# The state-space scan of a Mamba-2 block ahead of a routed MoE, laid out anew

## The chip, the cores and the metric

The kernel runs on 1 core of one Trainium2 chip. The metric is the device time of one launch in microseconds (us): 385.34 as the median of 3 runs of the kernel before (384.26 to 385.63). TensorE has two clock levels, 1.2 and 2.4 GHz; the profile gives the granted clock as a share of full speed.

## The reference, cut to what matters

```
# x [4, 8, 768, 32], a [4, 8, 768], B, C [4, 8, 768, 16]: batch, head, step, ...
# chunks of 64 steps, per (batch, head):
cum   = cumsum(log(clip(a, 1e-6, 1)))                 # within a chunk
L     = exp(cum_i - cum_j) for i >= j, else 0
y     = (L * (C @ B^T)) @ x                           # inside a chunk
S'    = exp(cum_end) * S + (exp(cum_end - cum) * B)^T @ x    # state [16, 32]
y    += exp(cum) * C @ S                              # from the chunks before
tokens = y as [3072, 256]                             # heads side by side
e      = (token_id * 2654435761) % 8                  # expert of a token
out    = relu(tokens @ W1[e]) @ W2[e]                 # 256 -> 1024 -> 256, fp32
```

All data are fp32. There are 4 batches of 12 chunks of 64 steps and 8 heads, so 384 small scan problems, and then 8 experts with some 384 tokens each.

## The kernel before, in words

The kernel has two halves. The **scan** writes y to a DRAM tensor `y_tokens`; the **MoE** gathers the tokens of one expert at a time from it (L454), turns them (L477), multiplies with W1 and W2 (L489, L498), turns back (L515) and scatters the rows to the output (L459). The MoE is the same in both kernels, but for the moments at which weights are loaded.

In the scan a "chunk" of the program (`chunk(gc)`, 24 of them, 6 in a batch) is 128 steps, two of the reference's chunks, u = 0 and 1, one in each half of the partitions. Once a batch `prepare(b)` makes the operands:

- B and C lie as 128 rows of 6 steps each; DVE multiplies them with the decay factors (`rows`, L330), PE turns them with 12 transposes (L337), and ACT and DVE copy them out of PSUM (L340 to L344). `bt` and `ce` then have head and state (8 x 16) on the partitions and the steps along the row. `ce` has three copies: C of the even heads, of the odd heads, and whole.
- B is turned back by 6 transposes (L348) so that its steps lie on partitions, and 24 matmuls (L359) make the state that each 64 steps add, all 8 heads at once, of which 4 x 4 blocks of heads are computed and the diagonal is used. DVE runs the recurrence over 12 states (L372) and masks each one to the diagonal (`up`, L375).

A chunk has 8 "grams" (L393: 64 x 64 decayed C B^T for two heads each, 8 tiles of PE), a causal mask by DVE (`m`, L396), 4 "z" matmuls (L405, the part from the earlier states), copied to SBUF by ACT (L407), 16 "y" matmuls (L413), and DVE's sum of the two (L416), which one DMA writes out (L417).

Once, after the second chunk, `invert()` (L293 to L316) turns the expert slots of the tokens into lists for the gathers: two POOL operations on one-hot tables (L302, L304) and 24 matmuls (L307).

What sets the order: the functions are called in the order of the loop at L419 to L440, and a scheduler then arranges the instructions on each engine by its own estimates. One SP queue issues all loads and the writes of y; POOL issues the gathers and scatters. There are five weight buffers (`NWB = 5`); L109 and L111 load W1 and W2 of an expert.

Of the kernel before, what the change touches and what calls it, by code (L numbers as in the profile page):

```python
# [9 lines left out]
F32 = mybir.dt.float32  # L10
# [10 lines left out]
def kernel(  # L21
# [11 lines left out]
    nc = tc.nc  # L33
# [12 lines left out]
    NWB = 5  # L46
# [27 lines left out]
    awork = pool(a_ctx, "awork", 2)  # L74
    ps_t = pool(a_ctx, "ps_t", 2, space=PSUM)
    ps_g = pool(a_ctx, "ps_g", 2, space=PSUM)
    ps_y = pool(a_ctx, "ps_y", 2, space=PSUM)


    a_t = apre.tile([P, SQ], F32)  # L80
    nc.sync.dma_start(out=a_t, in_=a.rearrange("b h (q t) -> (b h q) t", q=Q))
# [39 lines left out]
    causal = const.tile([P, G, HL], F32)  # L121
    for u in range(2):
        nc.vector.tensor_copy(out=causal[u * HL:(u + 1) * HL],
                              in_=upto[0:HL, 0:HL].unsqueeze(1).to_broadcast([HL, G, HL]))
    turn0 = const.tile([P, UQ, HL], F32)
    nc.vector.memset(turn0, 1.0)
    nc.vector.memset(turn0[:, :, 0:1], 0.0)
# [15 lines left out]
    selq = const.tile([P, Q, BH], F32)
    nc.vector.tensor_copy(out=selq, in_=ident.rearrange("p (j q) -> p q j", q=Q))
    mbq = apre.tile([P, NB, Q], F32)
    nc.vector.tensor_reduce(out=mbq, in_=idv.rearrange("p b h q -> p b q h"), axis=AX.X, op=OP.add)
    mh = apre.tile([P, H], F32)
    nc.vector.tensor_reduce(out=mh, in_=idv.rearrange("p b h q -> p h b q"), axis=AX.XY, op=OP.add)
    mhn = apre.tile([P, H, NS], F32)
    nc.vector.tensor_copy(out=mhn, in_=mh.unsqueeze(2).to_broadcast([P, H, NS]))  # L150
# [4 lines left out]
    cum = apre.tile([P, UQ, HL], F32)  # L155
    nc.vector.tensor_tensor_scan(out=cum.rearrange("p u t -> p (u t)"), data0=turn0.rearrange("p u t -> p (u t)"),
                                 data1=a_t, initial=0.0, op0=OP.mult, op1=OP.add)
    mid = cum[:, :, HL // 2 - 1:HL // 2]
    rel = apre.tile([P, UQ, HL], F32)
    nc.vector.tensor_tensor(out=rel, in0=cum, in1=mid.to_broadcast([P, UQ, HL]), op=OP.subtract)  # L160
    fac = apre.tile([P, 2, SQ], F32)
    relf = rel.rearrange("p u t -> p (u t)")
    nc.scalar.activation(fac[:, 0], relf, AF.Exp, scale=-1.0)
    nc.scalar.activation(fac[:, 1], relf, AF.Exp)
    fac_ps = ps_t.tile([P, 2, R, BH], F32, name="tp")
    for i in range(2):
        for r in range(R):
            for q in range(Q):
                nc.tensor.matmul(out=fac_ps[q * PQ:(q + 1) * PQ, i, r],
                                 lhsT=fac[:, i].rearrange("p (t r) -> p r t", r=R)[:, r], rhs=selq[:, q],  # L170
                                 start=True, stop=True)
    dec = const.tile([P, 2, R, BH], F32)
    nc.vector.tensor_copy(out=dec, in_=fac_ps)

    ends = apre.tile([P, 2, UQ], F32)
    nc.vector.tensor_copy(out=ends[:, 0], in_=mid.rearrange("p u o -> p (u o)"))
    nc.vector.tensor_copy(out=ends[:, 1], in_=rel[:, :, HL - 1])
    endb = apre.tile([P, 2, NB * Q, UQ], F32)
    for i in range(2):
        nc.vector.tensor_tensor(out=endb[:, i], in0=ends[:, i].unsqueeze(1).to_broadcast([P, NB * Q, UQ]),  # L180
                                in1=mbq.rearrange("p b q -> p (b q)").unsqueeze(2).to_broadcast([P, NB * Q, UQ]),
                                op=OP.mult)
    end_ps = ps_t.tile([P, 2, NB, NU], F32, name="tp")
    nc.tensor.matmul(out=end_ps.rearrange("p i b u -> p (i b u)"), lhsT=mhn.rearrange("p h n -> p (h n)"),
                     rhs=endb.rearrange("p i c u -> p (i c u)"), start=True, stop=True)
    step = const.tile([P, NB, NU], F32)
    nc.vector.tensor_copy(out=step, in_=end_ps[:, 0])
    nc.vector.tensor_tensor(out=step[:, :, 1:], in0=step[:, :, 1:], in1=end_ps[:, 1, :, 0:NU - 1], op=OP.add)
    nc.scalar.activation(step, step, AF.Exp)
# [22 lines left out]
    def routing():  # L212

        assert E == 8 and 2654435761 % E == 1
# [24 lines left out]

        start = route.tile([P, E], F32)  # L240
# [7 lines left out]
                                op0=OP.logical_shift_right)  # L248
        tiles = route.tile([P, E], F32)
# [5 lines left out]

        base = route.tile([P, E], F32)
# [358 lines left out]
```

## Time and profile before

| | us |
|---|---|
| median of 3 runs | 385.34 |
| the profiled execution | 384.65 |
| its span, first to last instruction | 382.9 |
| first y leaves (L417) | 29.9 |
| last y leaves (L417) | 159.93 |
| first matmul of expert 0 (L489) | 170.72 |

The span has three stages: start and scan (0 to 159.93), the first gathers (to 170.72), and the MoE. Two of PE's records per fp32 matmul are to be expected: it is done in two passes, so a count of 768 at L413 is 384 matmuls. The mean duration of a matmul record includes time in which other tiles of PE run beside it; what a group costs is read from its start to the start of the next group. The `PEclk` row is the granted clock where the trace has a record of it.

### The profile page before, as it was taken

What the parts mean: (1) busy time and instruction counts of PE and PEld (TensorE: products, weight loads), DVE (VectorE), ACT (ScalarE), POOL (GpSimd) and SP (SyncE); (2) the same over time, 40 slices, a digit from 0 to 9 for tenths busy, and PEclk for the clock granted to TensorE, in tenths of its full rate; (3) what the DMA queues carried; (4) which work ended last, traced back from release to release, by engine and by line L of the source; (5) the groups of instructions that cost most, each with busy time, mean ns of one, the idle gap of its engine ahead of it and who ended that gap; (6) DMA issues with size and microseconds to landing.
All of it is one profiled execution on the core that took longest, in us unless ns stands there. A gap on an engine that the chain in (4) does not pass through costs nothing.

```text
span 382.9 us, 5947 instructions
## 1 busy us (share of the span) xinstructions
PE 330.9 (86%) x2375; PEld 214.2 (56%) x2375; DVE 126.5 (33%) x328; ACT 67.6 (18%) x142; POOL 71.7 (19%) x85
## 2 busy tenths in 40 slices
PE   2688688999898888549999999999999999999950
PEld 2466557778776776525555555555555555555520
DVE  6769644544733453111121211212122131211210
ACT  3500043043034211101111011010110201111110
POOL 2001400000000000074212605216043120211230
PEclk9999999999999855557999999999999999999985
DMA  9977564739440000122033441432011000000100
GB/s 163 168 122 230 157 176 90 223 92 268 154 132 29 15 29 29 41 74 63 27 127 123 128 164 55 144 123 68 4 43 43 14 27 0 29 14 0 45 27 16
DMA packets 50256, 33.29 MB, mean 87 GB/s; under 512 B 35087, under 2 KB 46505, under 8 KB 50228
## 3 DMA queue, kind: packets, MB, share of 16 engines
q1 hardware_dynamic: 47412, 26.34, 26.0%
q0 software_dynamic: 2816, 6.56, 5.4%
q8 instruction: 19, 0.31, 0.3%
q14 instruction: 9, 0.07, 0.1%
HBM read 26.60 MB, written 6.55 MB: 87 GB/s over the span
## 4 chain that ended last, share of the span: by engine, by line
PE 57%; issue 17%; DMA 7%; DVE 7%; POOL 5%; SPq 2%; ACT 2%; POOLq 0%; DVEq 0%
PE h_ps L489 15%; PE o_ps L498 14%; PE y_ps L413 9%; DMA out_dram<-o_sb,idx_out 5%; PE gram L405 5%; PE tp L359 4%; PE gram L393 4%; POOL out_dram L459 2%; PE tp L337 2%; DVE m L396 2%; SPq L94 2%; PE tp L348 2%; PE xt_ps L477 1%; DMA bc<-in_B_dram 1%; DVE v L372 1%
## 5 line engine op out<-in xcount | busy, mean ns | idle before, releaser
L489 PE MATMUL h_ps<-xT,w 128*128 128x416 f32 x256 | 102.4, 525 | 0.4 <-DVE xT L478 0.4
L498 PE MATMUL o_ps<-hT,w 128*128 128x416 f32 x256 | 102.1, 518 | 0.0
L498 PEld LDWEIGHTS o_ps<-hT,w 128*128 128x128 f32 x256 | 47.5, 190 | 40.1 <-issue 36.3
L489 PEld LDWEIGHTS h_ps<-xT,w 128*128 128x128 f32 x256 | 47.4, 195 | 32.7 <-issue 31.5
L413 PE MATMUL y_ps<-x_t,m 64*64 64x32 f32 x768 | 64.0, 287 | 0.0
L413 PEld LDWEIGHTS y_ps<-x_t,m 64*64 64x64 f32 x768 | 60.1, 215 | 0.0
L459 POOL DMA_INDIRECT out_dram<-o_sb,idx_out x32 | 31.2, 975 | 114.1 <-ACT o_sb L518 95.8
L454 POOL DMA_INDIRECT xg<-y_tokens,idx_in x32 | 32.0, 1000 | 94.4 <-issue 63.5
L405 PE MATMUL gram<-up,ce 64*64 64x128 f32 x192 | 34.0, 437 | 12.8 <-DVE m L396 10.5
L484 DVE TENSOR_SCALAR hT<-h_ps 128x416 f32<-128x416 f32 x32 | 18.9, 592 | 75.1 <-PE h_ps L489 75.1
L478 DVE COPY xT<-xt_ps 128x256 f32<-128x256 f32 (+1 forms) x32 | 12.0, 375 | 71.1 <-PE xt_ps L477 71.1
L482 ACT ACTIVATE hT<-h_ps 128x416 f32<-128x416 f32 x32 | 16.5, 517 | 97.3 <-PE h_ps L489 97.3
L405 PEld LDWEIGHTS gram<-up,ce 64*64 64x64 f32 x192 | 16.7, 204 | 23.3 <-DVE m L396 15.4
L407 ACT ACTIVATE z_sb<-gram 128x128 f32<-128x128 f32 x48 | 13.2, 277 | 88.7 <-PE gram L405 64.5
L393 PE MATMUL gram<-ce,bt 32*64 32x128 f32 x384 | 25.9, 435 | 0.0
L416 DVE TENSOR_TENSOR y_sb<-y_ps,z_sb 128x256 f32<-128x256 f32 x24 | 10.2, 424 | 38.5 <-ACT z_sb L407 22.8
L477 PEld LDWEIGHTS xt_ps<-ident,xg 128*128 128x128 f32 (+1 forms) x64 | 8.4, 148 | 21.7 <-issue 19.6
L359 PE MATMUL tp<-x_t,bs 64*64 64x128 f32 x192 | 20.0, 427 | 0.0
L477 PE MATMUL xt_ps<-ident,xg 128*128 128x128 f32 (+1 forms) x64 | 12.6, 280 | 8.5 <-issue 6.6
L396 DVE TENSOR_TENSOR m<-gram,causal 128x256 f32<-128x256 f32 x48 | 18.9, 417 | 3.2 <-PE gram L393 3.1
L375 DVE SCALAR_TENSOR_TENSOR up<-v,step,own 128x128 f32<-128x128 f32 x44 | 18.9, 429 | 0.5
L359 PEld LDWEIGHTS tp<-x_t,bs 64*64 64x64 f32 x192 | 16.0, 217 | 2.0 <-issue 1.3
(117 smaller groups left out, 186.6 us busy)
## 6 DMA issues: line engine op xcount, KB each, us to landing
w<-in_moe_w_dram SPq DMA_DIRECT2D x16, 1024.0 KB, 5.7
x_t<-in_x_dram SPq DMA_DIRECT2D x24, 128.0 KB, 4.2
y_tokens<-y_sb SPq DMA_DIRECT2D x24, 128.0 KB, 1.8
bc<-in_B_dram SPq DMA_DIRECT2D x4, 384.0 KB, 4.5
bc<-in_C_dram SPq DMA_DIRECT2D x4, 384.0 KB, 4.8
xg<-y_tokens,idx_in POOLq DMA_INDIRECT x32
out_dram<-o_sb,idx_out POOLq DMA_INDIRECT x32
a_t<-in_a_dram SPq DMA_DIRECT2D x1, 96.0 KB, 2.1
```

The source lines that it names most:

```text
L359: nc.tensor.matmul(out=d_ps[u][q * HL:(q + 1) * HL, c - c0], lhsT=bs[u * HL:(u + 1) * HL, c, q * HL:(q + 1) * HL], rhs=xs[b * R + c][u * H ...
L375: nc.vector.scalar_tensor_tensor(out=up[:, k + 1].rearrange("p g d -> p (g d)"), in0=v, scalar=step[:, b, k + 1:k + 2], in1=own.rearrange( ...
L393: nc.tensor.matmul(out=gram[u * HL:(u + 1) * HL, k, 0:P], lhsT=bt[r, t], rhs=ce[r, 0:2, t], start=True, stop=True)
L396: nc.vector.tensor_tensor(out=m.rearrange("p (k e) i -> p k (e i)", k=2), in0=gram[:, :, 0:P], in1=causal.rearrange("p (k e) i -> p k (e i ...
L405: nc.tensor.matmul(out=gs[q][u * HL:(u + 1) * HL, 0, P:2 * P], lhsT=ce[rq, 2, t], rhs=up[rq, 2 * c + u].rearrange("p g d -> p (g d)"), sta ...
L413: nc.tensor.matmul(out=y_ps[w, h * D:(h + 1) * D], lhsT=ms[q][w, k], rhs=x_t[w, h], start=True, stop=True)
L454: nc.gpsimd.indirect_dma_start(out=dst, out_offset=None, in_=y_dram[:], in_offset=bass.IndirectOffsetOnAxis(ap=idx, axis=0), bounds_check= ...
L459: st = nc.gpsimd.indirect_dma_start(out=out[:], out_offset=bass.IndirectOffsetOnAxis(ap=idx, axis=0), in_=src, in_offset=None, bounds_chec ...
L477: nc.tensor.transpose(out=tp[:, i, 0:r], in_=g[0:r, i * P:(i + 1) * P], identity=ident[0:r, 0:r])
L484: nc.vector.tensor_scalar_max(out=o, in0=i, scalar1=0.0)
L489: nc.tensor.matmul(out=hp, lhsT=w1s[e][:, i, f * P:(f + 1) * P], rhs=xT[e][:, i], start=(i == 0), stop=(i == DP - 1))
L498: nc.tensor.matmul(out=oP[e][:, j, 0:CAP], lhsT=w2s[e][:, f, j * P:(j + 1) * P], rhs=h, start=(f == 0), stop=(f == FP - 1))
```

## The change

The scan is written anew between the loads and `a_ctx.close()`; the same sums are formed from other tiles.

- **Order.** A manual schedule holds around the scan: instructions stay on each engine as the program has them. The grams of the next chunk come before the outputs of this one; a preparation of the next batch is spread over the six chunks of a batch, the routing over some twenty.
- **Loads.** B and C lie as 96 rows of 8 steps (512-byte pieces) in one buffer, x by head with the heads 0 to 3 in the lower 64 partitions and 4 to 7 in the upper (8 DMAs a batch in place of 6; 16 for the first batch), a as 96 rows with pieces of 32 bytes.
- **B by steps.** The decayed B goes from SBUF to a DRAM tensor and comes back with steps on partitions (`put_steps`, `get_steps`); the 6 transposes that turned it back and their copies go. C and B take 8 transposes of 96 rows each.
- **States.** 44 matmuls per batch of 32 x 64 outputs (pairs of heads) in place of 24 of 64 x 128; DVE's recurrence works on 64 columns; POOL masks them in two operations (`blocks`).
- **Grams.** Still 8 matmuls per chunk, but both u of a pair of heads go to the same partitions, side by side; four tiles of PE in place of eight. One DVE operation masks all.
- **Outputs.** z is the first matmul of a PSUM accumulation and y is added to it; the two head halves have a bank each. One ACT copy replaces two ACT copies and a DVE sum. Two DMAs write it.
- **Start.** Matmuls on constants (`spin`) stand between the first operations of PE.
- **Weights.** Four buffers in place of five.

The diff, cut to its core:

```diff
-    NWB = 5
+    NWB = 4
-    ps_y = pool(a_ctx, "ps_y", 2, space=PSUM)
+    ps_y = pool(a_ctx, "ps_y", 1, space=PSUM)
+    scan_order = tc.manual_schedule()
+    scan_order.__enter__()
+    a_t = apre.tile([NR, BH, RS], F32)
+    nc.sync.dma_start(out=a_t, in_=a.rearrange("b h (p r) -> p (b h) r", r=RS))
...
+    def load_x(b, parts=1):
+        t = aload.tile([P, NU, G, D], F32, name="x_t", bufs=3)
+        for u in range(parts):
+            us = slice(u * NU // parts, (u + 1) * NU // parts)
+            for h in range(H):
+                q, k = divmod(h, G)
+                nc.sync.dma_start(out=t[q * HL:(q + 1) * HL, us, k],
+                                  in_=x[b, h].rearrange("(u j) d -> j u d", j=HL)[:, us])
...
+    def spin(moving, n=1):
+        t = ps_y.tile([P, 2, 512], F32, name="y_ps")
+        for _ in range(n):
+            nc.tensor.matmul(out=t[:, 0, 0:moving.shape[-1]], lhsT=ident[0:moving.shape[0]], rhs=moving, ...)
+    spin(ones, 10)
...
+    def rows(b, i, eng):
+        t = abat.tile([NR, RS, P], F32, name="rows", bufs=2)
+        eng.tensor_tensor(out=t.rearrange("p r (h n) -> p h r n", h=H), in0=bcs[b][:, i],
+                          in1=fac[:, i, b * H:(b + 1) * H].unsqueeze(3).to_broadcast([NR, H, RS, NS]), op=OP.mult)
+    def put_steps(b):
+        nc.sync.dma_start(out=b_dram[b].rearrange("(p r) n -> p r n", r=RS), in_=rws[b, 0])
+    def get_steps(b):
+        t = abat.tile([P, NU, HL], F32, name="bs")
+        for q in range(2):
+            nc.sync.dma_start(out=t[q * HL:(q + 1) * HL],
+                              in_=b_dram[b].rearrange("(k j) (q n) -> q j k n", j=HL, q=2)[q])
...
+    def turned(b, i):
+        t = rws.pop((b, i))
+        for r0 in (0, RS // 2):
+            tp = ps_t.tile([P, 512], F32, name="tp")
...
+                nc.tensor.transpose(out=v[:, r], in_=t[:, r0 + r], identity=ident[0:NR, 0:NR])
...
+    def turn_c(b):
+        ct = abat.tile([P, NU, RS, RU], F32, name="ct", bufs=1)
+        for r0, v in turned(b, 1):
+            nc.scalar.activation(ct[:, :, r0:r0 + RS // 2].rearrange("p k r c -> p r k c"), v, AF.Copy)
...
+        for e in range(2):
+            nc.vector.tensor_scalar(out=ce[:, e], in0=c3, scalar1=par[:, e:e + 1], scalar2=None, op0=OP.mult)
+        nc.gpsimd.tensor_tensor(out=cp, in0=c3, in1=step[:, b].unsqueeze(2).to_broadcast([P, NU, HL]), op=OP.mult)
+    def states(b, half):
+        for i in range(n):
+            k = half * UH + i
+            for r in range(G):
+                q, g = divmod(r, 2)
+                w = slice(q * HL, (q + 1) * HL)
+                nc.tensor.matmul(out=tp[32 * r:32 * r + 32, i * PW:(i + 1) * PW], lhsT=bs[w, k, 32 * g:32 * g + 32],
+                                 rhs=xb[w, k, 2 * g:2 * g + 2].rearrange("p h d -> p (h d)"), start=True, stop=True)
...
+                nc.vector.scalar_tensor_tensor(out=st[:, k + 1], in0=st[:, k], scalar=step[:, b, k:k + 1],
+                                               in1=tp[:, i * PW:(i + 1) * PW], op0=OP.mult, op1=OP.add)
+    def blocks(b, k0, k1):
+        nc.gpsimd.tensor_tensor(out=ups[b][:, k0:k1], in0=sts[b][:, k0:k1]..., in1=own..., op=OP.mult)
...
-        for q in range(2):
-            gram = ps_g.tile([P, 2, 512], F32, name="gram")
-            for k in range(2):
-                r = slice(32 * (2 * q + k), 32 * (2 * q + k) + 32)
-                for u in range(2):
-                    nc.tensor.matmul(out=gram[u * HL:(u + 1) * HL, k, 0:P], lhsT=bt[r, t], rhs=ce[r, 0:2, t], ...)
+    def grams(gc):
+        gram = ps_g.tile([P, 2, 512], F32, name="gram")
+        for u in range(2):
+            for r in range(G):
+                q, g = divmod(r, 2)
+                rr = slice(32 * r, 32 * r + 32)
+                nc.tensor.matmul(out=gram[q * HL:(q + 1) * HL, g, u * P:(u + 1) * P],
+                                 lhsT=bts[b][rr, 2 * c + u].rearrange("p c r -> p (c r)"), rhs=ces[b][rr, :, 2 * c + u], ...)
+        nc.vector.tensor_tensor(out=m..., in0=gram[:, :, 0:2 * P], in1=causal..., op=OP.mult)
+    def outputs(gc):
+        y_ps = ps_y.tile([P, 2, 512], F32, name="y_ps")
+        for q in range(2):
+            for u in range(2):
+                if k:
+                    nc.tensor.matmul(out=y_ps[u * HL:(u + 1) * HL, q, 0:P], lhsT=cps[b][w, k],
+                                     rhs=ups[b][w, k].rearrange("p g x -> p (g x)"), start=True, stop=False)
+        for h in range(G):
+            for q in range(2):
+                for u in range(2):
+                    nc.tensor.matmul(out=y_ps[u * HL:(u + 1) * HL, q, h * D:(h + 1) * D], lhsT=m[w, g, u, e],
+                                     rhs=xs[b][w, k, h], start=(k == 0 and h == 0), stop=(h == G - 1))
+        nc.scalar.activation(y_sb, y_ps[:, :, 0:P], AF.Copy)
+        for u in range(2):
+            t0 = gc * P + u * HL
+            nc.sync.dma_start(out=y_dram[t0:t0 + HL, :].rearrange("(p r) d -> r p d", r=RS),
+                              in_=y_sb[u * HL:(u + 1) * HL].rearrange("p q d -> p (q d)"))
...
+    for gc in range(NCH):
+        if gc + 1 < NCH:
+            grams(gc + 1)
+        outputs(gc)
+        if gc == 0:
+            states(0, 1)
+            blocks(0, UH + 1, NU)
+        next(todo, None)
+        if c == 0:
+            rows(nb, 0, nc.gpsimd)
+            rows(nb, 1, nc.gpsimd)
+            if nb + 1 < NB:
+                load_x(nb + 1)
+        elif c == 1:
+            put_steps(nb)
+            turn_b(nb)
+            if nb + 1 < NB:
+                load_bc(nb + 1)
+        elif c == 2:
+            get_steps(nb)
+            turn_c(nb)
+        elif c == 3:
+            states(nb, 0)
+        elif c == 4:
+            states(nb, 1)
+            blocks(nb, 1, UH + 1)
+            if b == 1:
+                load_w(0)
+            elif b == 2:
+                load_w(1)
+        else:
+            blocks(nb, UH + 1, NU)
+    for _ in todo:
+        pass
+    load_w(2)
```

How PE's order moves. First PE in the kernel before, in the first batch, after the inversion: grams (L393), transposes for the preparation (L337, L348), z (L405), y (L413) and states (L359).

```order
L393 MATMUL gram<-ce,bt 64x128 x8
L337 MATMUL tp<-ident,rows 128x128
L405 MATMUL gram<-up,ce 64x128 x2
L413 MATMUL y_ps<-x_t,m 64x32 x5
L405 MATMUL gram<-up,ce 64x128 x2
L413 MATMUL y_ps<-x_t,m 64x32 x11
L337 MATMUL tp<-ident,rows 128x128 x5
L393 MATMUL gram<-ce,bt 64x128
L337 MATMUL tp<-ident,rows 128x128 x3
L393 MATMUL gram<-ce,bt 64x128
L337 MATMUL tp<-ident,rows 128x128 x3
L393 MATMUL gram<-ce,bt 64x128 x6
```

And PE in the changed kernel, from the second chunk of batch 1 on: z is L471, y L480, grams L454, transposes L389, states L426.

```order
L454 MATMUL gram<-ce,bt 64x128 x8
L471 MATMUL y_ps<-up,cp 64x128 x4
L480 MATMUL y_ps<-x_t,m 64x32 x16
L389 MATMUL tp<-ident,rows 128x96 x8
L454 MATMUL gram<-ce,bt 64x128 x8
L471 MATMUL y_ps<-up,cp 64x128 x4
L480 MATMUL y_ps<-x_t,m 64x32 x16
L389 MATMUL tp<-ident,rows 128x96 x8
L454 MATMUL gram<-ce,bt 64x128 x8
L471 MATMUL y_ps<-up,cp 64x128 x4
L480 MATMUL y_ps<-x_t,m 64x32 x16
L426 MATMUL tp<-x_t,bs 32x64 x24
```

In the kernel before, the grams of a chunk are directly followed by its own z and y, which need the mask made of them; now a whole chunk's z and y stand between the grams and the outputs that need them, and the transposes and states of the next batch stand between two chunks.

SP in the kernel before, in the first batch: the writes of y (L417) with the loads of x (L94), weights (L109, L111) and B and C (L88) among them.

```order
L417 DMA y_tokens<-y_sb 128x256
L94 DMA x_t<-in_x_dram 128x8x32
L109 DMA w_974<-in_moe_w_dram 128x2x1024
L417 DMA y_tokens<-y_sb 128x256
L94 DMA x_t<-in_x_dram 128x8x32 x2
L417 DMA y_tokens<-y_sb 128x256
L111 DMA w_976<-in_moe_w_dram 128x8x256
L88 DMA bc<-in_B_dram 128x8x96
L88 DMA bc<-in_C_dram 128x8x96
L417 DMA y_tokens<-y_sb 128x256
```

SP in the changed kernel, over the first batch: L487 writes y, L373 puts the decayed B of the next batch into DRAM, L379 fetches it by steps.

```order
L487 DMA y_tokens<-y_sb 8x8x256 x2
L101 DMA x_t<-in_x_dram 64x12x32 x8
L487 DMA y_tokens<-y_sb 8x8x256 x2
L373 DMA b_steps<-rows 96x1024
L90 DMA bc<-in_B_dram 96x8x128
L90 DMA bc<-in_C_dram 96x8x128
L487 DMA y_tokens<-y_sb 8x8x256 x2
L379 DMA bs<-b_steps 64x12x64 x2
L487 DMA y_tokens<-y_sb 8x8x256 x4
```

The round trip of B stands between writes of y: the put behind the second chunk's, the get behind the third's, and the get waits on this queue for the put to land.

## Rows read from the trace of the kernel before

**Rows 1.** The profile's page: its first line and the granted clock in 40 slices.

```profile
span 382.9 us, 5947 instructions
...
PEclk9999999999999855557999999999999999999985
```

**Rows 2.** Stretches: length, busy (x) of PE, PEld, DVE, ACT, POOL; PEclk, DMA, GB/s.

```profile
0.00:29.90 29.90, 18.21 (x221) 13.41 (x221) 20.11 (x79) 10.52 (x16) 2.24 (x17) 1.00 0.87 146
29.90:71.65 41.75, 34.01 (x394) 26.60 (x391) 24.51 (x50) 8.74 (x18) 6.08 (x3) 1.00 0.63 177
71.65:159.93 88.28, 78.41 (x1129) 64.50 (x1124) 40.66 (x113) 21.52 (x52) 0.20 (x1) 0.84 0.32 95
159.93:170.72 10.79, 2.40 (x9) 1.19 (x9) 1.50 (x4) 0.00 (x0) 6.21 (x6) 0.50 0.22 64
170.72:382.90 212.18, 197.85 (x632) 108.45 (x632) 39.73 (x84) 26.81 (x56) 56.99 (x58) 0.96 0.18 59
```

**Rows 3.** Timeline of one chunk: start, us, engine, line, records [idle before <-releaser].

```profile
113.74 0.48 PE L405 MATMUL gram<-up,ce 64*64 64x128 f32 x2
...
116.29 0.73 PE L393 MATMUL gram<-ce,bt 32*64 32x128 f32 x16
...
116.95 0.47 PE L337 MATMUL tp<-ident,rows 128*128 128x128 f32 x1
117.06 0.75 DVE L396 TENSOR_TENSOR m<-gram,causal 128x256 f32<-128x256 f32 x2 [0.18 <-PE gram L393]
...
117.54 0.48 PE L405 MATMUL gram<-up,ce 64*64 64x128 f32 x2
```

**Rows 4.** Timeline of PE where four and where eight of its tiles work together.

```profile
116.29 0.52 PE L393 MATMUL gram<-ce,bt 32*64 32x128 f32 x8
...
5.29 1.67 PE L169 MATMUL tp<-selq,fac 128*32 128x32 f32 x96 [5.29 <-ACT fac L163]
```

**Rows 5.** The clock: two stretches, L413 around 115 and 129, grams at 152.

```profile
110.00:120.00 10.00, 9.77 (x155) 8.39 (x154) 2.36 (x6) 2.99 (x8) 0.00 (x0) 1.00 0.10 34
150.00:160.00 10.00, 8.35 (x144) 7.28 (x142) 2.78 (x7) 1.64 (x6) 0.00 (x0) 0.50 0.08 28
...
L413 PE MATMUL y_ps<-x_t,m 64*64 64x32 f32 x25 | 1.8, 290 | 0.0
L413 PE MATMUL y_ps<-x_t,m 64*64 64x32 f32 x28 | 1.2, 226 | 0.0
...
151.73 0.73 PE L393 MATMUL gram<-ce,bt 32*64 32x128 f32 x16
...
155.52 0.73 PE L393 MATMUL gram<-ce,bt 32*64 32x128 f32 x16
```

**Rows 6.** Groups by line: busy us, mean ns of one, idle before and releaser.

```profile
L359 PE MATMUL tp<-x_t,bs 64*64 64x128 f32 x192 | 20.0, 427 | 0.0
L337 PE MATMUL tp<-ident,rows 128*128 128x128 f32 x48 | 14.9, 440 | 0.3 <-ACT bt L340 0.3
L330 DVE TENSOR_TENSOR rows<-bc,dec 128x768 f32<-128x768 f32 x8 | 7.6, 955 | 4.5 <-PE tp L337 3.4 <-DMA bc<-in_B_dram 0.9
L340 ACT ACTIVATE bt<-tp 128x384 f32<-128x384 f32 x8 | 6.5, 864 | 11.0 <-PE tp L337 10.9
L304 POOL TENSOR_SCALAR of<-of,one_up 128x1272 bf16<-128x1272 bf16 x1 | 3.5, 3541 | 0.0
L302 POOL TENSOR_TENSOR of<-of,iota_b 128x1272 bf16<-128x1272 bf16 x1 | 2.3, 2345 | 34.0 <-DVE of L300 34.0
```

**Rows 7.** SP's DMAs: landing of y and B; issue of x in ns, min/median/max.

```profile
y_tokens<-y_sb SPq DMA_DIRECT2D x24, 128.0 KB, 1.8
bc<-in_B_dram SPq DMA_DIRECT2D x4, 384.0 KB, 4.5
...
L94 SPq DMA_DIRECT2D x_t<-in_x_dram x24: 367/714/2352, 3.2 to 90.1; - x24
```

**Rows 8.** Timeline at the start: the wait for a, and eight loads of x.

```profile
2.91 0.26 DVE L153 TENSOR_SCALAR a_t<-a_t 128x192 f32<-128x192 f32 x1 [1.51 <-DMA a_t<-in_a_dram]
...
11.29 8.64 SPq L94 DMA_DIRECT2D x_t<-in_x_dram  x8
```

More of the change, by code (lines that the diff above doesn't have):

```diff
@@ L143 @@
[L143 to L150, printed above, removed]
+    turn0 = const.tile([NR, BH, RS], F32)
@@ L153 @@
+    nc.vector.memset(turn0, 1.0)
+    nc.vector.memset(turn0[:, :, 0:1], 0.0)
+    def spin(moving, n=1):
+        t = ps_y.tile([P, 2, 512], F32, name="y_ps")
+        for _ in range(n):
+            nc.tensor.matmul(out=t[:, 0, 0:moving.shape[-1]], lhsT=ident[0:moving.shape[0]], rhs=moving,
+                             start=True, stop=True)
+    spin(ones, 10)
     nc.vector.tensor_scalar(out=a_t, in0=a_t, scalar1=1e-6, scalar2=1.0, op0=OP.max, op1=OP.min)
     nc.scalar.activation(a_t, a_t, AF.Ln)
-    cum = apre.tile([P, UQ, HL], F32)
@@ L164 @@
[L164 to L182, printed above, removed]
@@ L183 @@
[L183 to L189 removed]
+    cum = apre.tile([NR, BH, RS], F32)
@@ new lines @@
+    flat = lambda t: t.rearrange("p c r -> p (c r)")
+    nc.vector.tensor_tensor_scan(out=flat(cum), data0=flat(turn0), data1=flat(a_t), initial=0.0,
+                                 op0=OP.mult, op1=OP.add)
+    tot = apre.tile([NR, BH], F32)
+    nc.vector.tensor_copy(out=tot, in_=cum[:, :, RS - 1])
+    rel_ps = ps_t.tile([P, 512], F32, name="tp")
+    nc.tensor.matmul(out=rel_ps[0:NR, 0:BH], lhsT=rel_w.rearrange("p k r -> p (k r)"), rhs=tot, start=True, stop=True)
+    off = apre.tile([NR, BH], F32)
@@ new lines, in steps @@
+    def steps():
+        step_ps = ps_t.tile([P, 512], F32, name="tp")
+        for b in range(NB):
+            nc.tensor.matmul(out=step_ps[:, b * NU:(b + 1) * NU],
+                             lhsT=totx[:, b * H:(b + 1) * H].rearrange("p h n -> p (h n)"), rhs=step_w,
+                             start=True, stop=True)
+        nc.scalar.activation(step.rearrange("p b k -> p (b k)"), step_ps[:, 0:NB * NU], AF.Exp)
+    par = const.tile([P, 2], F32)
+    own = const.tile([P, 2, 2, D], F32)
@@ L422 @@
+    rows(0, 0, nc.vector)
+    put_steps(0)
+    get_steps(0)
+    rows(0, 1, nc.gpsimd)
+    heads()
+    turn_b(0)
+    steps()
+    spin(ones, 2)
+    load_bc(1)
+    turn_c(0)
+    spin(ones, 4)
+    grams(0)
+    states(0, 0)
+    blocks(0, 1, UH + 1)
+    load_x(1)
+    todo = iter(routing())
     for gc in range(NCH):
         b, c = divmod(gc, R)
-        if c == 0 and b + 1 < NB:
-            for i in range(R):
-                load_x((b + 1) * R + i)
-        if c == 0 and 0 < b < NB - 1:
-            load_bc(b + 1)
```

276 lines of the change are left out of this document (130 added, 146 removed).

## The prediction, made before the result was known

> **What bounds the kernel now.** I read the stretches first [rows 2]. Up to the last write of y at 159.93 PE is busy for 18.2 of 29.9, 34.0 of 41.8 and 78.4 of 88.3 us, and no other engine comes near it (DVE 40.7 of 88.3): the scan is bound by PE, at 0.89 of its time at the end. The 222 us behind it are the gathers and the MoE, which the change leaves alone. So the question is how many us of PE a chunk and a preparation cost. I take the span of 382.9 [rows 1] with the 1.75 around it as 384.65; that is 0.2% under the median of 385.34, so the forecast gets 0.7 added at the end.
>
> Then one chunk in the timeline [rows 3]. It runs from its first z at 113.74 to the next chunk's at 117.54, 3.8 us: z and y 2.55 (to 116.29), grams 0.66 (to 116.95), then 0.59 in which PE does one transpose and waits for the mask, which DVE starts at 117.06. The last batch has 6 chunks and no preparation, the two batches before it 12 and two, so 88.28 less 18 x 3.8 leaves 9.9 for each preparation. Batch 0 has 41.75: five chunks 19.0, a preparation 9.9, and 12.8 for the inversion of the routing, for which PE stands.
>
> Last the clock, since every PE duration hangs on it [rows 5]. The stretch 110 to 120 is shown at 1.00 and 150 to 160 at 0.50, but 16 gram records take 0.73 in both [rows 3, 5], and the chunk from 151.73 to 155.52 takes 3.79: the same. Around 129 a y record takes 226 ns in place of 290. So the 1.00 before 128 is no reading, the scan runs at 1.2 GHz nearly throughout, and it does so with PE busy 9.77 of 10 us.
>
> **The chunk.** z and y are 8 and 32 records (two passes each). In 2.55 us that is 64 ns for one, with two tiles of PE beside each other, or 128 ns of one tile. The order h, q, u lets four quadrants work at once, so 32 ns: 40 x 32 = 1.28. That four tiles do overlap is seen at L169, 96 records in 1.67 us, 17 ns each [rows 4]. The tile's shape changes between z, y and grams; I add 0.2 for it (bounds 0 and 0.45). If only two tiles overlap still, the 2.55 stays. The grams were eight tiles, whose first passes start together [rows 4], so two rounds and the way through the array are 0.66, a third of it each, 0.22. Now four tiles need four rounds: 0.66 + 0.44 = 1.1. The wait for the mask goes, since the grams are made a chunk ahead; what is late next is the single ACT copy from the one y buffer, which has the next grams' 1.1 us to hide in. 1.28 + 0.2 + 1.1 = 2.6 us, against 3.8.
>
> **Preparation, on PE.** 88 state records of 64 columns: half a round, 0.11, over four tiles, 2.4 us, with 0.25 at the end of each half 2.9 (4.8 if two tiles overlap). Those of before are 192 in four batches [rows 6], twice as wide. 16 transposes of 96 columns, at 0.22 for 128: 2.7. Changes of mode 1.0. Together 6.6 against 9.9 (bounds 5 and 9). Beside it, a batch of 22 us has on POOL two `rows` of 1024 columns, `cp` 768, `blocks` 768 and 640; at L302's 1.84 ns a column [rows 6] that is 7.8. DVE has six masks of 0.75 (two halves in [rows 3]), `ce` 2 x 0.96 as L330, some 4 for the states: 10. ACT has four copies as L340, 3.5, and six for y at two thirds of it, 3.5: all inside 22 us.
>
> **B through DRAM.** SP issues the get behind the y of the third chunk of a batch; PE wants it after the transposes of C and one more chunk, 1.4 + 2.6 = 4.0 later. The nearest landings are 1.8 (y, 128 KB) and 4.5 (B, 384 KB) [rows 7]; a get is twice 192 KB, so I take 3.5 and count nothing; at the upper bound 0.5 is lost, three times. If PE became twice as fast, the cover would be 2 us and 1 to 2.5 would show each time.
>
> **Start.** a arrives now in 3072 pieces of 32 bytes. It set the beginning at 2.91 [rows 8]; 8192 pieces of x took 8.64, so at most 3.2 later. The factors need fewer steps after it, but B's two trips (1.8 to 4.5 each) stand before the first states. x has 6144 pieces for batch 0, as many as before. I take the first y at 26 (23 to 31), against 29.9.
>
> **Sum.** Batch 0 behind its first chunk: 5 x 2.6, a preparation 6.6, its own second half of states 1.4, routing steps on PE 1.5: 22.5, to 48.5. Then 18 x 2.6 + 2 x 6.6 = 60.0, and the inversion, which is now spread out; its 24 matmuls (2.3) stand one chunk behind POOL's 5.9 [rows 6], so PE waits 0 to 3.3 for them and I take 1.7: 4.0. Last y at 112.5, 47.4 earlier. The third and fifth weight loads now go out beside the first gathers: +1 (0 to 3, within one landing of [rows 7]). 384.65 − 47.4 + 1 = 338.2, with 0.7 for the median 339.
>
> **Rivals.**
> - *A, the clock rises.* Against it: 98% busy at 1.2 GHz [rows 5]. For it: a chunk streams the same columns in 2.6 us as in 3.8, 1.45 times as dense, which no chunk of before was. The Trainium skill (TensorE: Matmul & The Clock Gate, Part 1: The HAM clock gate) says that the slow clock is the default and that sustained matmul work releases it; the 98% above speaks against reading "sustained" as PE's busy share. At 2.4 GHz PE's chunk would be 1.3, and z, y and the one ACT copy in a chain make 1.5; a batch 9 + 3.4 + 1.6 of waits = 14; last y at 25 + 17 + 2 x 14 + 9 + 4 = 83, 77 earlier: 384.65 − 77 + 1.7 = 309 (300 to 324).
> - *B, the fixed order waits.* POOL, ACT's copy of the one y buffer, or the get are late in each batch, since nothing moves ahead of them on PE. For it: in the kernel before, a scheduler placed PE's work around such waits. At 5 us a batch: 339 + 15 = 354 (348 to 370).
> - *D, tiles that share a PSUM bank take turns.* Now the grams of two row tiles lie in one bank, and the states of both. The grams would take twice four rounds, +0.88 a chunk, 21 in all, the states +2.4 in four batches, 10: 339 + 31 = 370. Against it: y before put both row tiles into one bank, and its records came every 62 ns (25 in the 1.56 us before 116.28 [rows 3, 5]), as z's do. The Trainium skill (TensorEngine Tiling (Array Packing), Restrictions and Gotchas) says that different row tiles cannot access the same bank at the same time; L169's four tiles have one row tile, so they don't decide it.
> - *S, slower.* In order, PE stands behind the whole DRAM trip in each of three batches: SP issues eight x loads at up to 2.35 each [rows 7], 19 us, in front of the put, then two trips and the load of B and C at 4.5 each, 14: 33 behind a cover of 12, so 21 late, 63 in all against the gain of 47: 401. It decides from 16 us a batch. Against it: the median issue is 0.71, and x lands in a buffer free long before.
>
> **Chances.** My forecast, the clock low nearly all the time, 0.43 (326 to 352 by its bounds); A 0.33; B 0.14; D 0.05; S 0.04; that the fixed order gives back all but 2 us of the gain, 0.01. The range 302 to 360 leaves out the lowest of A, the highest of B, D and S, some 0.2. A measurement of this kernel tells 0.5% from no change; faster by more is my forecast, A, B and D, 0.95; within it 0.01; slower 0.04.
>
> **What would show it.** Chunks 2.6 apart by their first z; L480's records at 32 ns; 1.1 from the first gram to the next line; no wait of PE for L458's mask; states waiting under 0.5 for the get; first y near 26, last near 112. Chunks of 2.6 beside a granted clock of 0.50 say that the clock stayed low. I am wrong if L480 stays at 64 ns (two tiles), if chunks are 1.5 apart (A), or if PE's idle time has POOL, ACT or a DMA as its releaser (B, S).

## The result, and the profile after

The changed kernel takes 355.54 us (median of 4 runs, 353.37 to 358.53) against 385.49 on the same chip: ratio 0.923 [0.916, 0.931], 30 us faster. Run again beside the experiments it had 0.931 [0.923, 0.938]. The forecast of 339 had the direction, but of 46 us forecast, 30 came. 355.5 lies in the range of 302 to 360, yet 16 us above the point and above the 326 to 352 that the forecast's own terms allowed: the range held because it took in rival B. From here on times are medians, and like the ratios they are taken over those runs of a kernel that lie within 1.5% of its fastest.

The page of the changed kernel, first line and granted clock, and its stretches, cut where those of [rows 2] are cut (first y, second batch, last y, expert 0); columns as there:

```profile
span 354.4 us, 6033 instructions
...
PEclk9855555656757885699999999999999999999985
```

```profile
0.00:30.52 30.52, 17.30 (x202) 14.90 (x205) 11.76 (x24) 6.03 (x10) 13.69 (x33) 0.75 0.81 129
30.52:59.11 28.59, 21.35 (x418) 17.61 (x409) 16.34 (x37) 4.24 (x8) 8.96 (x6) 0.50 0.54 113
59.11:128.29 69.18, 49.08 (x1216) 40.32 (x1212) 42.12 (x74) 12.29 (x27) 24.22 (x13) 0.68 0.53 142
128.29:142.82 14.53, 2.43 (x9) 1.16 (x9) 1.50 (x4) 0.00 (x0) 8.75 (x9) 0.60 0.96 319
142.82:354.40 211.58, 197.75 (x632) 108.47 (x632) 39.83 (x84) 26.84 (x56) 54.40 (x56) 0.96 0.21 70
```

The MoE is as long as before (211.6 against 212.2). The last y leaves at 128.3, 31.6 earlier, where 47.4 were forecast; the way from there to expert 0 is 14.5 in place of 10.8. In the third stretch PE is busy 49 of 69 us, 0.71: in [rows 2] it was 0.89. So PE is no longer what binds, and the next thing to read is what it waits for. PE's waits from 30 to 128, by the line that waited and what ended the wait (total, times, longest; `issue` means that the profile shows no releaser):

```profile
PE tp L426 <- issue: 10.4, 3, 8.2
PE y_ps L480 <- DVE m L458: 4.2, 3, 2.0
PE tp L243 <- DVE eid_r L241: 3.4, 1, 3.4
PE tp L346 <- POOL of L342: 3.1, 1, 3.1
PE tp L426 <- DMA bs<-b_steps: 2.2, 3, 1.4
PE tp L254 <- DVE mask L250: 1.1, 1, 1.1
PE tp L389 <- ACT bt L399: 0.9, 1, 0.9
PE y_ps L471 <- ACT y_sb L484: 0.6, 1, 0.6
```

Together 26 us. Half of it, 12.6, stands before the states (L426), whose operand is what comes back from DRAM. The timeline of PE shows one chunk at each clock level, and the longest wait (start, us, records):

```profile
56.62 1.13 PE L454 MATMUL gram<-ce,bt 32*64 32x128 f32 x16
57.68 0.70 PE L471 MATMUL y_ps<-up,cp 64*64 64x128 f32 x8
58.16 1.02 PE L480 MATMUL y_ps<-x_t,m 64*64 64x32 f32 x32
59.11 1.13 PE L454 MATMUL gram<-ce,bt 32*64 32x128 f32 x16
...
80.88 0.51 PE L426 MATMUL tp<-x_t,bs 64*32 64x64 f32 x4 [8.24 <-issue]
...
122.69 0.67 PE L454 MATMUL gram<-ce,bt 32*64 32x128 f32 x16
...
124.13 0.67 PE L454 MATMUL gram<-ce,bt 32*64 32x128 f32 x16
```

A chunk is 2.49 us where the granted clock is 0.50 (56.62 to 59.11) and 1.44 where it is full (122.69 to 124.13), against 3.80 before [rows 3]. The terms of the chunk came out: grams 1.06, z and y 1.43, no wait for the mask in a free chunk. SP's timeline around the longest wait says where the get of B was:

```profile
63.51 6.39 SPq L101 DMA_DIRECT2D x_t<-in_x_dram  x8
70.00 1.30 SPq L487 DMA_DIRECT2D y_tokens<-y_sb  x2
71.39 0.38 SPq L373 DMA_DIRECT2D b_steps<-rows  x1
71.88 0.37 SPq L90 DMA_DIRECT2D bc<-in_B_dram  x1
72.30 0.95 SPq L90 DMA_DIRECT2D bc<-in_C_dram  x1
73.34 1.27 SPq L487 DMA_DIRECT2D y_tokens<-y_sb  x2
75.02 1.44 SPq L379 DMA_DIRECT2D bs<-b_steps  x2
```

POOL had made the rows by 64.05 (run 6 shows the line), but eight loads of x took SP until 69.9, and the write of the second chunk's y stood behind them; the put went out 7.3 us after its rows were ready. The states began at 80.9, 4.4 after the get had been issued, with the next B and C (768 KB) ahead of it. From 74 to 80 the 16 DMA engines were busy throughout (share 1.06, 218 GB/s), so the landing is a part of this wait, beside the order on SP.

### The profile page after: what moved, and what is told of

It reads as the page before. It is cut to its first block, busy times and chain, and to the rows that moved or that the text cites. A ratio compares the mean times of both kernels' runs of the same rounds, so it can differ in the third digit from the quotient of the medians.

```text
span 354.4 us, 6033 instructions
## 1 busy us (share of the span) xinstructions
PE 287.9 (81%) x2461; PEld 182.5 (51%) x2461; DVE 111.6 (31%) x222; ACT 49.4 (14%) x101; POOL 110.0 (31%) x115
## 4 chain that ended last, share of the span: by engine, by line
PE 45%; issue 20%; DMA 14%; DVE 9%; POOL 5%; SPq 4%; ACT 1%; POOLq 0%; ACTq 0%; DVEq 0%
PE h_ps L595 16%; PE o_ps L604 15%; DMA out_dram<-o_sb,idx_out 6%; DMA bs<-b_steps 3%; DVE st L433 3%; POOL out_dram L565 3%; PE y_ps L480 2%; PE gram L454 2%; PE tp L426 2%; DMA xg<-y_tokens,idx_in 2%; SPq L101 2%; PE xt_ps L583 2%; DMA bc<-in_C_dram 2%; PE tp L389 1%; PE y_ps L471 1%
## 5 line engine op out<-in xcount | busy, mean ns | idle before, releaser
L595 PEld LDWEIGHTS h_ps<-xT,w 128*128 128x128 f32 x256 | 47.4, 195 | 32.5 <-issue 30.8
L584 DVE COPY xT<-xt_ps 128x256 f32<-128x256 f32 (+1 forms) x32 | 12.0, 375 | 77.6 <-PE xt_ps L583 77.6
L426 PE MATMUL tp<-x_t,bs 64*32 64x64 f32 x352 | 13.3, 308 | 17.0 <-issue 10.4
L441 POOL TENSOR_TENSOR up<-st,own 128x768 f32<-128x768 f32 (+1 forms) x8 | 13.4, 1672 | 44.2 <-DVE st L433 44.2
L454 PE MATMUL gram<-ce,bt 32*64 32x128 f32 x384 | 23.3, 379 | 2.2 <-DVE ce L409 2.2
L480 PE MATMUL y_ps<-x_t,m 64*64 64x32 f32 x768 | 21.4, 257 | 4.2 <-DVE m L458 4.2
L480 PEld LDWEIGHTS y_ps<-x_t,m 64*64 64x64 f32 x768 | 21.6, 184 | 5.1 <-DVE m L458 5.1
L583 PE MATMUL xt_ps<-ident,xg 128*128 128x128 f32 (+1 forms) x64 | 12.6, 280 | 13.0 <-DMA xg<-y_tokens,idx_in 12.0
L583 PEld LDWEIGHTS xt_ps<-ident,xg 128*128 128x128 f32 (+1 forms) x64 | 8.4, 147 | 26.2 <-issue 23.0
L484 ACT ACTIVATE y_sb<-y_ps 128x256 f32<-128x256 f32 x24 | 9.2, 384 | 89.5 <-PE y_ps L480 86.2
L458 DVE TENSOR_TENSOR m<-gram,causal 128x512 f32<-128x512 f32 x24 | 16.4, 685 | 16.4 <-PE gram L454 16.4
L426 PEld LDWEIGHTS tp<-x_t,bs 64*32 64x32 f32 x352 | 10.6, 164 | 18.7 <-issue 16.4
L454 PEld LDWEIGHTS gram<-ce,bt 32*64 32x64 f32 x384 | 15.0, 184 | 5.3 <-DVE ce L409 2.4
L471 PE MATMUL y_ps<-up,cp 64*64 64x128 f32 x176 | 14.4, 384 | 3.4 <-POOL up L441 2.7
L626 ACT ACTIVATE o_sb<-ot_ps 128x256 f32<-128x256 f32 x16 | 6.1, 384 | 60.2 <-PE ot_ps L623 60.2
```

The lines of the kernel that those rows point to most:

```text
L426: nc.tensor.matmul(out=tp[32 * r:32 * r + 32, i * PW:(i + 1) * PW], lhsT=bs[w, k, 32 * g:32 * g + 32], rhs=xb[w, k, 2 * g:2 * g + 2].rearr ...
L454: nc.tensor.matmul(out=gram[q * HL:(q + 1) * HL, g, u * P:(u + 1) * P], lhsT=bts[b][rr, 2 * c + u].rearrange("p c r -> p (c r)"), rhs=ces[ ...
L458: nc.vector.tensor_tensor(out=m.rearrange("p g u e i -> p g (u e i)"), in0=gram[:, :, 0:2 * P], in1=causal.rearrange("p (g x) r c -> p g ( ...
L471: nc.tensor.matmul(out=y_ps[u * HL:(u + 1) * HL, q, 0:P], lhsT=cps[b][w, k], rhs=ups[b][w, k].rearrange("p g x -> p (g x)"), start=True, s ...
L480: nc.tensor.matmul(out=y_ps[u * HL:(u + 1) * HL, q, h * D:(h + 1) * D], lhsT=m[w, g, u, e], rhs=xs[b][w, k, h], start=(k == 0 and h == 0), ...
L583: nc.tensor.transpose(out=tp[:, i, 0:r], in_=g[0:r, i * P:(i + 1) * P], identity=ident[0:r, 0:r])
```

## The experiments

Theory: PE's waits are the shortfall, and most of them come from an order that lets nothing pass: on SP (x ahead of the put of B), on DVE and POOL (routing steps, tables). Rivals: the DMAs' landing itself; a chunk term that was mis-sized; DVE's load. Ratios are to the kernel before on the same chip. The changed kernel itself ran beside 2 to 4; 5 to 8 and 9 to 12 ran on two other chips, where its 0.923 and 0.931 stand in for it.

**1. The changed kernel again.**

> The changed kernel once more, for the comparisons of this chip. Theory (waits of the fixed order): 355 again, with PE standing about 8 us before the states of batch 2 and the first y near 30.5. Rival (the place and size of the waits are chance of one execution): other waits of other sizes.

Measured: 355.74, 0.931 [0.923, 0.938]. The waits before the states are 5.9 (batch 2) and 4.5 (batch 3), together 10.5, as 8.2 and 1.8 were; the longest one for the mask is 3.75, where it was 2.0. The places stay, the sizes wander by 2 to 3 us, so an edit worth 2 us isn't told by one profile.

**2. x behind the get.**

```diff
         if c == 0:
             rows(nb, 1, nc.gpsimd)
-            if nb + 1 < NB:
-                load_x(nb + 1)
...
         elif c == 3:
             states(nb, 0)
+            if nb + 1 < NB:
+                load_x(nb + 1)
```

> The eight x loads of a batch are issued behind the get of B (at the fourth chunk) and no longer ahead of the put. Theory (SP's queue order makes B late): the 8.6 us before the states of batch 2 go down to under 2, and the kernel is 5 to 9 us faster than the changed one, about 348. Rival (the trip through DRAM itself is too slow for the two chunks it has): the wait stays at 6 us or more, time within 2 us of 355.

Measured: 353.28, 0.923 [0.917, 0.929]; 2.5 below the changed kernel's own run beside it, with intervals that overlap. So the time is the rival's, while the wait of batch 2 (2.5) is neither the theory's (under 2) nor the rival's (6 or more). SP's put for batch 2, and PE's rows before the y that waits for its mask and before the states of batches 2 and 3:

```profile
68.22 0.37 SPq L373 DMA_DIRECT2D b_steps<-rows  x1
...
65.29 1.08 PE L480 MATMUL y_ps<-x_t,m 64*64 64x32 f32 x32 [3.76 <-DVE m L458]
...
76.82 0.51 PE L426 MATMUL tp<-x_t,bs 64*32 64x64 f32 x4 [2.52 <-issue]
...
100.81 0.51 PE L426 MATMUL tp<-x_t,bs 64*32 64x64 f32 x4 [3.11 <-DMA bs<-b_steps]
```

The long wait goes from 8.2 (5.9 in the repeat) to 2.5, so its place on SP was the cause of 3 to 6 us of it; all waits before the states go from 12.6 (12.5) to 8.2. It does not vanish: the put still goes out at 68.2 (71.4), because it stands behind the write of the second chunk, whose y had waited 3.8 for its mask; from there to the issue of the get it is 4.0, and from the get to the states 3.3. Batch 3, where no x was in the way, waits 3.1. And PE's waits for masks grow from 4.2 (4.8) to 7.6, so that all its waits together are 25.1 in place of 25.9.

**3. Half of batch 0's x behind the first get.**

```diff
         for u in range(parts):
+            if u:
+                yield
...
-    load_x(0, 2)
+    x0 = load_x(0, 2)
+    next(x0)
...
     put_steps(0)
     get_steps(0)
+    list(x0)
```

> Half of batch 0's x loads are issued behind the put and get of its B. Theory (the put, whose rows were ready near 10.3 and which went out at 15.3, stood behind 16 x loads): put near 10.5, first states some 4 us earlier, first y near 26.5, about 351. Rival (the get waits for the landing of the put and for a busy DMA, whatever the order): first y stays within 1.5 us of 30.5, about 355; a second one is that the later half of x becomes what is waited for, the same 355.

Measured: 354.05, 0.923 [0.917, 0.929]; 1.7 below, with intervals that overlap. Its SP and PE, with the line numbers moved by 3:

```profile
10.59 0.55 SPq L376 DMA_DIRECT2D b_steps<-rows  x1
...
31.53 1.30 SPq L490 DMA_DIRECT2D y_tokens<-y_sb  x2
```

The put goes out at 10.6 in place of 15.3 and the first z starts at 24.5 in place of 28.6. But the first y leaves at 31.5, no earlier, because SP is still issuing x of batch 1, and the next get then costs PE 4.1 where it had cost 1.4. The theory is right as to PE and wrong as to the end: two thirds of the 4 us go to the next wait.

**4. Weights inside the scan.**

```diff
         if nb is None:
+            if c < 2:
+                load_w(2 + c)
             continue
-    load_w(2)
...
-            if e == 0:
-                load_w(NWB - 1)
```

> The weights of experts 2 and 3 are loaded during the first two chunks of the last batch, and that of expert 4 only after expert 0: no weight load beside the first gathers. Theory (those loads slow the first gathers): from the last y to the first matmul of expert 0 14.5 goes back to about 11, total 352. Rival (the tail is longer because the last y leaves late, SP issuing two writes a chunk): the 14.5 stays, 355 or, with 4 MB more beside the last chunks' y, 356 to 358.

Measured: 357.79, 0.935 [0.929, 0.940], the rival's figure. From the first gather to the first turn of expert 0 (L583, here L584) it is 3.2 us (140.56 to 143.78), as in the kernel before (162.88 to 166.03), and 6.5 in the changed one (131.63 to 138.13): the loads did slow the gathers. From the last write of y to expert 0 it is 11.2 (137.1 to 148.3), which is the theory's figure. But SP's last writes of y now stand behind 4 MB:

```profile
124.18 0.46 SPq L115 DMA_DIRECT2D w<-in_moe_w_dram  x1
124.68 0.97 SPq L117 DMA_DIRECT2D w<-in_moe_w_dram  x1
125.75 11.87 SPq L487 DMA_DIRECT2D y_tokens<-y_sb  x8
```

PE's last y ended at 131.9, ACT's last copy waited 5.7 for a write of y to free its buffer, and the last write was issued at 137.1, 5.2 behind PE; in the changed kernel it was 1.2. What the gathers gained, the writes lost. (PE itself was 4.8 later here, 131.9 against 127.1; the last chunks ran at 0.50 here and at full clock there.)

**5. y with two tiles next to each other.**

```diff
-        for h in range(G):
-            g, e = divmod(h, 2)
-            for q in range(2):
+        for q in range(2):
+            for h in range(G):
+                g, e = divmod(h, 2)
```

> The y matmuls of a chunk are issued with the head half as the outer loop (q, h, u in place of h, q, u), so that two tiles of PE and not four stand next to each other in the order; nothing else. Theory (four quadrants halve y): the 32 y records of a chunk take about 2.0 us in place of 1.02 where the clock is low, chunks 3.4 to 3.5 us; over 24 chunks up to 20 us, of which waits elsewhere take some: 365 to 375. Rival (PE overlaps tiles whatever the order, or the waits of the scan set its length): 355 to 358.

Measured: 365.84, 0.953 [0.947, 0.959]: 10 us slower than the changed kernel. A chunk of it:

```profile
59.32 0.70 PE L471 MATMUL y_ps<-up,cp 64*64 64x128 f32 x8
59.80 1.47 PE L480 MATMUL y_ps<-x_t,m 64*64 64x32 f32 x32
61.20 1.13 PE L454 MATMUL gram<-ce,bt 32*64 32x128 f32 x16
```

y takes 1.40 (59.80 to 61.20) in place of 0.95. 24 x 0.45 = 10.8 is the size of the difference in time, but two more terms of this trace have to cancel for that: PE's waits from the first to the last y are 17.8 in place of 25.9, and some three chunks ran at full clock in place of nine. So four quadrants in turn pay against this order, by 0.45 a chunk, and not the 1.27 that halving the 2.55 of z and y had given them. z and y of this order take 1.88 (59.32 to 61.20). Where the other 0.67 down from 2.55 came from is not shown: z is no longer mixed into y, as it is in the kernel before (its order of PE), and the two tiles here lie on the same half of the rows, while those before lay on different halves.

**6. Rows on DVE.**

```diff
-            rows(nb, 0, nc.gpsimd)
-            rows(nb, 1, nc.gpsimd)
+            rows(nb, 0, nc.vector)
+            rows(nb, 1, nc.vector)
```

> The decayed B and C of batches 1 to 3 are made by DVE and not by POOL. Theory (small DVE operations stand still while POOL works on its rows, and so the mask comes late): no wait over 0.8 us for the mask L458 (1.6, 2.0 and 0.6 in the changed kernel), DVE's operations on 128x8 back to 0.2 us, rows some 2.6 us on DVE; 2 to 4 us faster than the changed kernel, about 352. Rival (the mask is late because DVE has too much to do in that chunk): the wait stays or grows by the 2.6, 355 to 358.

Measured: 355.24, 0.926 [0.921, 0.931], no change that can be told. First DVE and POOL in the changed kernel, then DVE in this one:

```profile
60.40 1.79 DVE L288 TENSOR_SCALAR jump<-jump 128x8 f32<-128x8 f32 x1
62.23 1.85 DVE L290 TENSOR_TENSOR jump<-jump,base 128x8 f32<-128x8 f32 x1
...
60.23 3.82 POOL L368 TENSOR_TENSOR rows<-bc,fac 96x1024 f32<-96x1024 f32 x2
```

```profile
58.72 1.13 DVE L285 TENSOR_SCALAR base<-iota_e 128x8 f32<-128x8 f32 x1
...
59.95 0.17 DVE L288 TENSOR_SCALAR jump<-jump 128x8 f32<-128x8 f32 x1
60.16 0.17 DVE L290 TENSOR_TENSOR jump<-jump,base 128x8 f32<-128x8 f32 x1
```

Two operations of 8 columns took 1.8 us each while POOL worked on its rows, and take 0.17 without them; the second one ended with POOL's, at 64.1. L285, which still runs beside POOL's `blocks` (to 59.8), keeps 1.13. So POOL does hold DVE up. But the mask is still waited for, 0.9, 0.5, 0.7 and 1.8, and PE now waits 0.8 and 1.3 for the rows on DVE: the theory is right about the cause and wrong about what it is worth.

**7. Routing earlier, inversion later.**

```diff
         yield
+        yield
         inv_ps = ps_t.tile([P, 512], F32, name="tp")[:, 0:2 * NK].rearrange("p (i x) -> p i x", i=2)
...
     steps()
+    todo = iter(routing())
+    next(todo)
...
     turn_c(0)
+    next(todo)
     spin(ones, 4)
     grams(0)
+    next(todo)
...
-    todo = iter(routing())
```

> The first three parts of the routing are issued before the first chunk, and the inversion's matmuls one chunk later behind POOL's tables. Theory (in a fixed order PE stands for whatever routing step comes first): the waits of 3.45 and 1.15 for the expert numbers and the mask of experts and of 3.15 for POOL go, first y stays near 30; 5 to 8 us faster, about 349. Rival (the time is only moved: the routing delays the first chunk by as much, or another wait such as the get of B takes it): within 2 us of 355.

Measured: 354.84, 0.923 [0.919, 0.928], the rival's. The three waits are gone from behind the first y (7.7 us), and others stand in their place; the first y itself leaves at 32.5 in place of 30.5. Three of them on PE, the mask here being that of the experts, now waited for ahead of the first y:

```profile
21.54 0.98 PE L254 MATMUL tp<-mask,ones 128*128 128x192 f32 x2 [3.72 <-DVE mask L250]
...
38.27 0.88 PE L390 MATMUL tp<-ident,rows 96*128 96x96 f32 x8 [2.66 <-POOL rows L369]
...
50.90 2.09 PE L427 MATMUL tp<-x_t,bs 64*32 64x64 f32 x48 [5.07 <-DMA bs<-b_steps]
```

**8. All edits.** The edits of 2, 3, 6 and 7, three weight buffers with the loads in batches 1 and 2, and on SP:

```diff
-            get_steps(nb)
             turn_c(nb)
+            if nb + 1 < NB:
+                load_bc(nb + 1)
...
             grams(gc + 1)
+        if c == 2 and nb is not None:
+            get_steps(nb)
         outputs(gc)
```

> All edits together: x loads behind the get, the next B and C behind it too, the get ahead of the third chunk's y, half of batch 0's x behind the first get, rows on DVE, routing earlier, inversion later, three weight buffers with no weight load between the last y and expert 0. Theory (PE's waits and the tail are the whole shortfall): the scan ends near 108 and expert 0 starts 11 us later, 332 to 338. Rival (a resource behind them, SP's queue or the landing of DMAs, holds the scan): 345 to 352, with PE waiting in other places.

Measured: 344.82, 0.898 [0.893, 0.902], some 11 us below the changed kernel; over the theory's 332 to 338 and at the lower edge of the rival's 345 to 352. PE's waits from 32 to 120, the largest four:

```profile
PE y_ps L475 <- ACT y_sb L488: 5.6, 3, 2.5
PE tp L430 <- DMA bs<-b_steps: 5.5, 4, 3.7
PE tp L393 <- DVE rows L372: 3.8, 2, 2.4
PE y_ps L475 <- POOL up L445: 3.4, 1, 3.4
```

The first y leaves at 34.0 (30.5 in the changed kernel), the last at 119.9, and expert 0 starts 11.3 later, which is nearly the 10.8 of before. One by one, x, the start, rows and routing gave 2.5, 1.7, 0 and some 1, none of them outside the intervals; with the tail's 3.2 that is 8 of the 11, and the moved get and the later B and C were not run alone. ACT's copy now waits where it had not: for a DMA of y, 4.1 and 5.1 us, as the writes are behind weights on SP.

**9. The three weight loads one batch apart.** In 8, the load of weights moves to the fourth chunk of batches 0 to 2 and x to the sixth.

> All edits, with the three weight loads put at the fourth chunk of batches 0 to 2 (behind the get) and x at the sixth. Theory (in the version with all edits the waits of 2.5 for ACT's copy and 3.7 for the get are y and B queued behind weights): those waits under 1 each, 339 to 341. Rival (the queue is as full wherever the weights stand): 344 to 346.

Measured: 343.42, 0.899 [0.892, 0.907], between the theory's 339 to 341 and the rival's 344 to 346, and no better than 8. PE's wait for the copy goes to 0.5, but PE stands 3.7 and 8.6 for the get of batches 2 and 3. So the theory does not hold: the wait takes another place.

**10. y issued by ACT.**

```diff
-            nc.sync.dma_start(out=y_dram[t0:t0 + HL, :]...
+            nc.scalar.dma_start(out=y_dram[t0:t0 + HL, :]...
```

> One edit on the changed kernel: the 48 writes of y are issued by ACT behind its copy, no longer by SP. Theory (what holds the scan is the single SP queue, in which B's put and get and the writes of y stand behind x and weight loads): the wait for the get in batch 2 under 4 us, first y leaves at 30, last y right behind PE's end; 4 to 8 us faster than the changed kernel, about 349. Rival (the landing of the DMAs, not their place in a queue): 353 to 357; a second rival is that ACT now stands for 1.3 us a chunk and its copies come late, 358 and over.

Measured: 361.91, 0.946 [0.940, 0.951], slower than the changed kernel by some 6. This theory falls. The time is in the second rival's range, but not by its reason: ACT does issue for 1.2 us a chunk, yet PE's waits for ACT's copies are 2.0 us in all, where the changed kernel has 1.5. What grew are the waits before the states (17.4, from 12.6) and for masks (8.8, from 4.2). SP without the writes, and PE's wait in batch 1:

```profile
21.69 21.52 SPq L101 DMA_DIRECT2D x_t<-in_x_dram  x16
48.35 0.33 SPq L373 DMA_DIRECT2D b_steps<-rows  x1
...
57.11 0.42 PE L426 MATMUL tp<-x_t,bs 64*32 64x64 f32 x4 [7.50 <-DMA bs<-b_steps]
```

16 loads of x go out in a row, up to 43.2; B's put of batch 1 follows at 48.4 where it had gone out at 39.3, and PE waits 7.5 and 1.9 for the get. What held the put from 43.2 to 48.4 the trace does not show. So the writes of y were not what stood in the way; that they had spread the loads is a reading of this view and was not tested by itself.

**11 and 12. y issued by ACT in the version of 9, and the DMA edits alone.** The second leaves rows on POOL and the routing where it was.

> The same with the writes of y issued by ACT. Theory (SP's queue): another 2 to 4 us, 336 to 338. Rival: the same as without it, within 1 us.

> Only the edits on DMAs: x and the next B and C behind the get, the get ahead of the third chunk's y, half of batch 0's x behind the first get, three weight buffers spread over the batches, y issued by ACT. Rows stay on POOL and the routing where it was. Theory (the DMA queue is the larger part of the shortfall, DVE, POOL and routing the smaller): 338 to 343. Rival (PE's waits for DVE and POOL are the larger part and remain, 10 us and more): 347 to 352.

Measured: 348.92, 0.909 [0.901, 0.916], and 352.11, 0.918 [0.910, 0.926]: the theory is wrong in both; 11 is not faster than 9 but slower, and 12 is at the upper edge of the rival's range. With y on ACT the version of 9 loses some 5 us, where the changed kernel had lost 6. Since 12 holds that loss too, it doesn't tell how much the DMA edits give without it; that stays open.

## Why the prediction was near and where it was off

- **The chunk, 2.6:** right, 2.49 (grams 1.06, z and y 1.43). Inside it the gain of four quadrants was put at 1.27; against the order of run 5 it is 0.45, and what gave the rest is open. The sum held, its reason is shown only in part.
- **Preparation, 6.6:** some 6.0 where nothing waits (states 1.5 to 2.0 and 1.2, two turns of 1.5). No row shows the 0.2 and the 1.0 for changes of tile shape by themselves.
- **"The wait for the mask goes", DVE and POOL "all inside 22 us":** each engine was counted alone. In the chunk where POOL makes the rows, DVE's operations stand beside it (run 6) and the mask comes late: 4.2 in three waits, 7.6 in run 2.
- **Start, 26:** 30.5. The failed step is that B's trip was counted by its landings and SP's order ahead of it not: the put, whose rows were ready near 10.3, stood behind 16 x loads until 15.3, and with that mended the first y stood behind the next 8 (run 3).
- **B through DRAM, "I take 3.5 and count nothing":** the step that failed most. 12.6 us of waits before the states, of which some 4 by the x loads ahead of the put (run 2); the 8 that stayed there are the trip, which takes 3.1 us or more from the put to the get's issue and 2 to 4.4 from there to the states, and what else stands ahead of it. Rival S had named this mechanism, with 21 us a batch; it was 8.2 once.
- **Routing, 1.5 and 1.7:** 7.7 of waits in the profile, but taking them away gave some 1 us, inside the intervals (run 7): the first y came 2 later, and the get was then waited for.
- **Tail, +1:** +3.7. The loads of weights doubled the time from the first gather to the first turn (6.5 against 3.2; run 4).
- **The clock:** the granted clock is 0.50 in batch 0 and 0.68 behind it, so A came true for about a third. Some nine chunks at 1.44 in place of 2.49 give back 9.5 us. From first to last y it is 97.8 against 86.5 forecast, +11.3: waits 25.9 less the 1.7 counted, less 9.5 by the clock, is 14.7, or 3.4 more than came. These 3.4 were not measured by themselves; 24 chunks 0.1 shorter and three preparations 0.6 shorter would give some 4.
- **The rivals:** B, the fixed order that waits, is what happened, at a chance of 0.14 against 0.43 for the forecast. That its 354 came so near is luck: the waits were 8 to 9 us a batch and not 5, and A's clock, which B left out, gave 9.5 back. Against D, grams of two row tiles in one bank take 1.06 for four rounds, not 1.98: here they do not take turns. The Trainium skill (TensorEngine Tiling (Array Packing), Restrictions and Gotchas) says that different row tiles cannot access the same bank at the same time; these 1.06 us go against it.

Not settled: what lets the clock rise. The granted clock goes from 0.50 to 1.00 four times: near 62.8, where PE had worked without a wait since 51.4, and near 86.7, 110.6 and 120.8, where it had worked for 5, 6 and 4 us behind a wait. It is back at 0.50 near 66.3, 93.5 and 117.4, 0.3 to 1.6 us after a wait of PE (1.6, 2.0 and 3.1 us) had ended.

## What to carry to other kernels

When the work of the busiest engine is made a third shorter, list what it will wait for in its own order, queue by queue, with everything that is issued ahead of each transfer, and not only the landing of that transfer. With the order fixed, a wait that is taken away mostly turns up at the next operand that is late: edits that gave 0 to 2.5 us alone, none clear of the spread, gave some 11 in one kernel with a few more. Moving writes out of a full queue need not free what stands behind them: here it cost 6 us.

## What had not been expected of the hardware

- POOL's large operations on SBUF hold up DVE's small ones: operations on 8 columns took 1.79 and 1.85 us beside POOL's rows, 0.17 without (run 6).
- With the weights of two experts loaded just before the gathers, the first turn comes 6.5 us after the first gather in place of 3.2 (run 4).
- A write of y in 64 rows of 1 KB in a turned order costs SP 0.58 us of issue (median of 48), and a chunk needs two; one of 128 rows in order had cost 0.34 (median of 24 in the kernel before).
